# State term on 64x64 array tiles in a fused linear-attention and ELU feed-forward kernel

## The chip, the cores and the metric

The kernel runs on one core of a Trainium2 chip. The metric is device time in microseconds (us). Five engines matter. PE is TensorE, the matmul array; its weight loads are a lane of their own (PEld). DVE is VectorE, ACT is ScalarE, POOL is GpSimd and SP is SyncE. Each engine takes its own instructions in the order in which they were written, and semaphores tie the engines together. POOL and SP also issue DMA transfers: POOL all loads that cast from fp32 to fp16, SP the stores and the DMA transposes.

## The reference

There are two stages: a causal linear attention with a decay per head, and an ELU feed-forward layer on its output.

```
q, k, v: (4, 8, 768, 64)   lam: (8)   w_in: (512, 2048)   w_out: (2048, 512)
for each block of the sequence:
    intra = (q k^T * Dmask) v              Dmask[i,j] = lam^(i-j) for i >= j, else 0
    inter = (q * lam^(i+1)) state
    out   = intra + inter
    state = lam^block * state + (k * lam^(block-1-i))^T v
x = out as (3072 tokens, 512 = 8 heads x 64)
h = x w_in ;  g = ELU(h) ;  result = g w_out          (fp32)
```

## The kernel before, in words

The sequence is cut into 6 blocks of 128 tokens, times 4 batches: 24 groups. Group g has block g // 4 and batch g % 4. Eight heads are four pairs hp of two heads hh. For a group these steps exist, and a single letter names each in the written order of the program (`OPEN`, lines 53 to 62, and the loop at lines 613 to 634):

- T: q and k are transposed on PE (groups 0 to 7), or by DMA from SP (W, groups 8 on).
- S: the scores, 8 matmuls of 64 rows by 128 columns of the array (line 310). One bank of PSUM per hh. DVE multiplies them by the decay mask into `pp` (line 326).
- P: the attention output, transposed (x^T), into a PSUM bank `psO`. Per head pair there are two value matmuls (line 346; all 128 rows, 64 columns of the array each) and, from block 1 on, two state matmuls (line 352). The state of a batch is a 128x128 matrix per head pair with the two heads' 64x64 states on its diagonal and zeros beside them, so that a state matmul also takes all 128 rows and 64 columns. Then ACT (groups 0 to 7) or DVE (line 369, multiplying by `qs`) writes `psO` to `xt` in SBUF. A block of 128 rows of `xt` holds heads 2hp and 2hp+1.
- U: the state's new part, k^T v (line 405 for groups 0 to 3: four matmuls on the whole array; line 414 for the others: 16 matmuls of 128 rows by 64 columns for two groups), and two DVE instructions of 64 partitions that add it to the decayed old state (lines 424 and 426).
- M: the decayed old state, two POOL instructions of 64 partitions per group (line 386). kd (line 187) is POOL's decayed k.
- `1:g:j`: the first feed-forward matmul mm1 (line 493), ACT's exp and relu (499, 503), DVE's join into `g` (468). `2:g:j`: the second one, mm2 (line 517).
- z and Z: zeros written into the state matrices, four by DVE (line 210) and four by ACT (line 553), since the blocks beside the diagonal must be zero.

From group 4 on two groups make a burst: before, its order on PE is U, U, P, P in the loop and P, P, U, U in `OPEN`. The scores of the pair after are set ahead of the burst in the loop. The PSUM banks are given by tag; in the loop the two `psO` of a burst use the two banks "H" that mm1's results use in turn.

Loads: POOL's queue issues, in the order of `POOL_ORDER` (line 47), q, k and v of each group and the weights. `emit_wi` (line 166) loads a slice of w_in of 256 columns as one transfer over 128 partitions, with four row blocks of 128 of w_in. wi0 to wi7 are these slices, wo0 to wo7 those of w_out. The eight semaphores of POOL's transfers are used in turn, so that an issue also waits until the transfer issued eight before it has landed. Among the issues stand POOL's own kd and M.

Of the kernel before, what the change touches and what calls it, by code (L numbers as in the profile page):

```python
# [14 lines left out]
def kernel(  # L15
# [37 lines left out]
    OPEN = (  # L53
# [11 lines left out]
        "S0=M0,M1 S1=C,D S2=D,M1 S3=D,B P0=M1 P1=B P2=B P3=D U0=M0 U1=D U2=A U3=M1 T0=M1,C T1=D,A "  # L65
        "T2=A,D T3=D T4=M0 T5=A T6=M1 T7=D M2=C M3=M0"
    )
# [25 lines left out]
    for i in range(7):  # L93
# [22 lines left out]
    st = [  # L116
        [cpool.tile([128, NHP, 128], FP16, name=f"st{b}_{i}") for i in range(2)]
        for b in range(B)
# [47 lines left out]
    def emit_wi(i):  # L166
        f0 = sum(WI[:i]) * 128
        nc.gpsimd.dma_start(  # L168
            out=wi16[i][:],
            in_=moe_w_in[:, f0 : f0 + WI[i] * 128].rearrange("(k p) f -> p k f", p=128),  # L170
        )

# [35 lines left out]

    def zero_st1(b):
        nc.vector.memset(st[b][1][:], 0.0)  # L210


    loglam = cpool.tile([128, H], FP32, name="loglam")
# [7 lines left out]
    mask = cpool.tile([128, H, 128], FP32, name="mask")  # L221
    qs = cpool.tile([128, NHP, 128], FP32, name="qs")
    ks = cpool.tile([128, H], FP32, name="ks")
    upp = cpool.tile([128, NHP], FP32, name="upp")
# [10 lines left out]
    def emit_qs():  # L235
        for hh in range(2):
            r = slice(hh * 64, (hh + 1) * 64)
            nc.vector.tensor_copy(loglam_p[r, :], loglam[r, hh::2])
        for hp in range(NHP):
            nc.scalar.activation(  # L240
                qs[:, hp, :], row[:], AF.Exp, scale=loglam_p[:, hp : hp + 1]
            )

# [57 lines left out]

    def att_S(g):
        qt, kt = qkT[g]
        psS[g] = [
            bank(f"S{g}", hh, [128, NHP, 128], FP32, f"psS{g}_{hh}") for hh in range(2)
        ]
        for hp in range(NHP):
            for hh in range(2):
                r = slice(hh * 64, (hh + 1) * 64)
                nc.tensor.matmul(  # L310
                    psS[g][hh][:, hp, :], lhsT=kt[r, hp, :], rhs=qt[r, hp, :],
                    start=True, stop=True,
                )

    late, X_done, Y_done, E_done = [], set(), set(), set()

    def until(done, g):
        while g not in done:
            late.pop(0)()

    def att_E(g):
# [11 lines left out]
        return [lambda: half(0), lambda: half(1)]  # L333

    def att_P(g):
        cb, b = divmod(g, B)
        until(E_done, g)
        if cb > 0:
            until(Y_done, g - B)
        vt = of(vg, g)  # L340
        qt, _ = qkT[g]
        po = bank(f"P{g}", 0, [128, NHP, 128], FP32, f"psO{g}")
        R = [slice(0, 64), slice(64, 128)]
        for hp in range(NHP):
            for hh, r in enumerate(R):
                nc.tensor.matmul(  # L346
                    po[r, hp, :], lhsT=vt[:, 2 * hp + hh, :], rhs=Pt[(g, hh)][:, hp, :],
                    start=True, stop=(cb == 0), skip_group_check=True,
                )
            if cb > 0:  # L350
                for r in R:
                    nc.tensor.matmul(  # L352
                        po[r, hp, :], lhsT=st[b][cb % 2][:, hp, r], rhs=qt[:, hp, :],
                        start=False, stop=True, skip_group_check=True,
                    )

        def evacuate():
            g0 = GFIRST[g]
            n = GSIZE[g0]
            if g0 not in xg:  # L360
                xg[g0] = asb.tile(
                    [128, NHP, n * 128], FP16, tag=f"xt{n}", name=f"xt{g0}",
                    bufs=4 if n == 1 else 2,
                )
            dst = xg[g0][:, :, (g - g0) * 128 : (g - g0 + 1) * 128]
            if g < GPE:
                nc.scalar.copy(out=dst, in_=po[:])  # L367
            else:
                nc.vector.tensor_tensor(out=dst, in0=po[:], in1=qs[:], op=ALU.mult)  # L369
            X_done.add(g)  # L370

        return [evacuate]

    stt = {}

    def att_M(g):
        cb, b = divmod(g, B)
        if cb == NCB - 1:
            return
        assert f"U{g - B}" in seen  # L380
        until(Y_done, g - B)
        old = st[b][cb % 2]
        for hh in range(2):
            r = slice(hh * 64, (hh + 1) * 64)
            tmp = asb.tile([128, NHP, 64], FP32, tag="stt", name=f"stt{g}_{hh}", bufs=8)
            nc.gpsimd.tensor_tensor(  # L386
                out=tmp[r], in0=old[r, :, r],
                in1=upp[r].unsqueeze(2).broadcast_to([64, NHP, 64]), op=ALU.mult,
            )
            stt[(g, hh)] = tmp  # L390

# [4 lines left out]
    def att_U(g, pu=None):  # L396

        cb, b = divmod(g, B)
        if cb == NCB - 1:
            return []  # L400
        vt = of(vg, g)
        if pu is None:
            full = bank(f"U{g}", 0, [128, NHP, 128], FP32, f"psU{g}")
            for hp in range(NHP):
                nc.tensor.matmul(
                    full[:, hp, :].rearrange("p (h e) -> p h e", h=2),
                    lhsT=kds[g][:, 2 * hp : 2 * hp + 2, :],
                    rhs=vt[:, 2 * hp : 2 * hp + 2, :], start=True, stop=True,
                )
        else:  # L410
            for hp in range(NHP):
                for hh in range(2):
                    r = slice(hh * 64, (hh + 1) * 64)
                    nc.tensor.matmul(  # L414
                        pu[r, hp, :], lhsT=kds[g][:, 2 * hp + hh, :], rhs=vt[:, 2 * hp + hh, :],
                        start=True, stop=True, skip_group_check=True,
                    )
        new = st[b][(cb + 1) % 2]

        def update(hh):  # L420
            r = slice(hh * 64, (hh + 1) * 64)
            src = full[r, :, r] if pu is None else pu[r, :, :]
            if cb == 0:
                nc.vector.tensor_copy(new[r, :, r], src)
            else:
                nc.vector.tensor_tensor(  # L426
                    out=new[r, :, r], in0=stt.pop((g, hh))[r], in1=src, op=ALU.add
                )
            if hh == 1:
                Y_done.add(g)  # L430

        return [lambda: update(0), lambda: update(1)]

    def burst(*ops):

        us = [int(o[1:]) for o in ops if o[0] == "U" and int(o[1:]) // B < NCB - 1]
        evs, ups, i = [], [], 0
        for o in ops:
            if o[0] == "P":
                evs += att_P(int(o[1:]))  # L440
# [110 lines left out]

    def zero_st(b):
        nc.scalar.memzero(st[b][0][:])

    def load_pair(g):
# [11 lines left out]
    def ready(t):  # L567

        g = int(t[1:])
        if t[0] == "P":  # L570
            assert g < B or f"U{g - B}" in seen
        if t[0] == "U" and g < 2 * B:
            assert f"{'z' if g < B else 'Z'}{g % B}" in seen
# [4 lines left out]
    def run(t):  # L578
        w, *a = t[0], *t[1:].replace(":", " ").split()
# [5 lines left out]
        a = [int(x) for x in a]  # L585
        if w in "PUzZ":
            ready(t)
        if w == "S":
            for g in a:
                att_S(g)  # L590
            for g in a:
# [9 lines left out]
        else:  # L601
            {"T": att_T_pe, "1": mm1, "2": mm2, "Z": zero_st, "z": zero_st1,
             "q": lambda g, e: cast_raw(g, "q", e), "k": lambda g, e: cast_raw(g, "k", e),
             "c": lambda i: (emit_qs, emit_mask, emit_ks)[i](), "W": pool_work, "L": load_pair,
             "M": next_M, "w": zero_matmuls}[w](*a)

# [27 lines left out]
    prog += m2  # L634
    for t in prog:
        run(t)
    mm2_rest()
# [33 lines left out]
```

## Time and profile before

| | us |
|---|---|
| median of 3 runs (lowest to highest) | 213.92 (212.92 to 214.82) |
| the profiled execution | 213.1 |
| its span, first to last instruction | 211.3 |
| PE busy | 203.1 |
| DVE / ACT / POOL busy | 135.7 / 127.9 / 98.6 |
| mm1 on PE (line 493), mm2 (line 517) | 97.9, 95.3 |
| PE idle before 21.5 us, from there to 48.0, from there to 201.0 | 5.3, 0.1, 0.0 |

The profile's page gives busy time by engine, the span in 40 slices, the chain of work that ended last, and the costliest groups of instructions by line. Matmuls are pipelined, so that what one costs is read from the distance between starts, not from its duration. For a DMA, the issue on its queue and the landing are two different times.

### The profile page before, as it was taken

Reading aid. Unit: us, or ns where it says so; the run is one execution under the profiler, and the core shown is the slowest. Engines: PE = TensorE matmul, PEld = TensorE weight load, DVE = VectorE, ACT = ScalarE, POOL = GpSimd, SP = SyncE. Lnnn points to the kernel's source line nnn. Section 1 sums busy time; section 2 is a strip of 40 time slices with the busy share of each in tenths; the row PEclk is TensorE's granted clock in tenths of the full one; section 3 lists DMA queues with packets and bytes.
Section 4 is the critical chain, followed back from the end, with each engine's and each line's share of the span. In section 5 each row is a group of like instructions: output and inputs, shape, how many; then the busy total and the mean of one; then the engine's idle time right before and its main releaser. Section 6 shows DMA issues by size and latency. Waiting matters only on the chain.

```text
span 211.3 us, 5116 instructions
## 1 busy us (share of the span) xinstructions
PE 203.1 (96%) x2072; PEld 139.3 (66%) x2072; DVE 135.7 (64%) x233; ACT 127.9 (61%) x245; POOL 98.6 (47%) x113
## 2 busy tenths in 40 slices
PE   7597999999999999999999999999999999999994
PEld 2365677768686766776766766766766766666653
DVE  6966454687837888679677777676676764433320
ACT  2747555874867756676476476476476477577640
POOL 8998990999873969249195279200000000000000
DMA  8999999999997699993999939996620110110112
GB/s 106 160 183 192 190 167 186 124 161 150 153 161 126 100 220 153 187 141 27 164 114 137 164 99 87 181 150 86 126 76 0 53 50 0 54 50 8 44 50 99
DMA packets 103079, 24.71 MB, mean 117 GB/s; under 512 B 93200, under 2 KB 100624, under 8 KB 103056
## 3 DMA queue, kind: packets, MB, share of 16 engines
q0 software_dynamic: 79760, 13.50, 83.7%
q1 hardware_dynamic: 22768, 10.76, 27.1%
q8 instruction: 16, 0.26, 0.6%
q10 hardware_dynamic: 528, 0.13, 0.3%
q14 instruction: 7, 0.06, 0.1%
HBM read 27.40 MB, written 6.29 MB: 159 GB/s over the span
## 4 chain that ended last, share of the span: by engine, by line
PE 88%; POOL 6%; DMA 3%; issue 0%; DVE 0%; POOLq 0%
PE psM L517 39%; PE psH L493 39%; DMA wo<-in_moe_w_out_dram 3%; PE psS L310 3%; PE psO L346 3%; PE psO L352 2%; POOL wi L168 1%; POOL kn L129 1%; POOL qn L129 1%; POOL vn L129 1%; PE psU L414 1%; PE psT L291 1%; POOL kd L187 0%; PE psMrest L529 0%; POOL wo L175 0%
## 5 line engine op out<-in xcount | busy, mean ns | idle before, releaser
L493 PE MATMUL psH<-xt,wi 128*128 128x256 f16 (+1 forms) x896 | 97.9, 257 | 0.7 <-ACT xt L367 0.6
L517 PE MATMUL psM<-wo,g 128*128 128x512 f16 (+1 forms) x384 | 95.3, 377 | 0.9 <-DMA wo<-in_moe_w_out_dram 0.9
L499 ACT ACTIVATE e<-psH 128x512 f32<-128x512 f32 x96 | 57.4, 598 | 64.0 <-PE psH L493 63.9
L493 PEld LDWEIGHTS <-wi 128*128 128x128 f16 x896 | 77.2, 98 | 24.1 <-DVE g L468 0.9
L468 DVE SCALAR_TENSOR_TENSOR g<-e,r 128x512 f16<-128x512 f32 x64 | 47.2, 738 | 40.2 <-ACT r L503 39.7
L517 PEld LDWEIGHTS <-g 128*128 128x128 f16 x384 | 36.4, 98 | 29.2 <-issue 1.2
L503 ACT ACTIVATE r<-psH 128x512 f32<-128x512 f32 x64 | 38.1, 595 | 0.0
L326 DVE TENSOR_TENSOR pp<-psS,mask 128x512 f16<-128x512 f32 x48 | 30.8, 684 | 3.0 <-PE psS L310 2.7
L468 DVE SCALAR_TENSOR_TENSOR g<-e,psH 128x512 f16<-128x512 f32 x32 | 21.9, 685 | 14.4 <-ACT psH L503 14.1
L386 POOL TENSOR_TENSOR stt<-st,upp 64x256 f32<-64x256 f16 x32 | 21.6, 674 | 17.0 <-DVE st L426 10.8
L187 POOL TENSOR_TENSOR kd<-kn,ks 128x512 f16<-128x512 f16 x20 | 21.3, 1067 | 16.0 <-DMA kn<-in_k_dram 14.5
L503 ACT ACTIVATE psH<-psH 128x512 f32<-128x512 f32 x32 | 19.1, 596 | 0.0
L543 ACT COPY osb<-psM 128x512 f32<-128x512 f32 (+1 forms) x24 | 14.1, 589 | 5.2 <-PE psM L517 5.2
L129 POOL DMA_DIRECT2D kn<-in_k_dram x14 | 15.5, 1108 | 0.8 <-POOLq L655 0.8
L129 POOL DMA_DIRECT2D vn<-in_v_dram x14 | 15.5, 1105 | 0.6 <-DMA wi<-in_moe_w_in_dram 0.6
L129 POOL DMA_DIRECT2D qn<-in_q_dram x13 | 14.7, 1131 | 0.0
L426 DVE TENSOR_TENSOR st<-stt,psU 64x256 f16<-64x256 f32 x32 | 13.3, 417 | 1.2 <-PE psU L414 0.5
L346 PE MATMUL psO<-pp,vn 128*64 128x128 f16 x192 | 11.9, 221 | 0.2 <-DVE pp L326 0.2
L369 DVE TENSOR_TENSOR xt<-psO,qs 128x512 f16<-128x512 f32 x16 | 10.5, 685 | 2.4 <-PE psO L352 2.3
L346 PEld LDWEIGHTS <-vn 128*64 128x64 f16 x192 | 9.8, 110 | 2.8 <-issue 2.5
L352 PE MATMUL psO<-qT,st 128*64 128x128 f16 x160 | 10.1, 219 | 0.0
L310 PE MATMUL psS<-qT,kT 64*128 64x128 f16 x192 | 8.0, 218 | 1.1 <-ACT kT L299 1.0
(48 smaller groups left out, 89.6 us busy)
## 6 DMA issues: line engine op xcount, KB each, us to landing
out_dram<-osb SPq DMA_DIRECT2D x19, 256.0 KB, 3.5
kn<-in_k_dram POOLq DMA_DIRECT2D x10, 256.0 KB, 7.5
qn<-in_q_dram POOLq DMA_DIRECT2D x10, 256.0 KB, 7.9
vn<-in_v_dram POOLq DMA_DIRECT2D x10, 256.0 KB, 7.6
wi<-in_moe_w_in_dram POOLq DMA_DIRECT2D x8, 256.0 KB, 6.8
wo<-in_moe_w_out_dram POOLq DMA_DIRECT2D x8, 256.0 KB, 7.5
out_dram<-osb SPq DMA_DIRECT2D x8, 128.0 KB, 1.8
kn<-in_k_dram POOLq DMA_DIRECT2D x4, 128.0 KB, 5.1
```

Source lines behind the costliest of these rows:

```text
L129: nc.gpsimd.dma_start(out=t[:].rearrange("p b h d -> p (b h) d"), in_=src)
L187: nc.gpsimd.tensor_tensor(out=kd[:], in0=of(kg, g), in1=ks[:].unsqueeze(2).broadcast_to([128, H, 64]), op=ALU.mult,)
L310: nc.tensor.matmul(psS[g][hh][:, hp, :], lhsT=kt[r, hp, :], rhs=qt[r, hp, :], start=True, stop=True,)
L326: nc.vector.tensor_tensor(out=P[:], in0=pts[hh][:], in1=mask[:, hh::2, :], op=ALU.mult)
L346: nc.tensor.matmul(po[r, hp, :], lhsT=vt[:, 2 * hp + hh, :], rhs=Pt[(g, hh)][:, hp, :], start=True, stop=(cb == 0), skip_group_check=True,)
L352: nc.tensor.matmul(po[r, hp, :], lhsT=st[b][cb % 2][:, hp, r], rhs=qt[:, hp, :], start=False, stop=True, skip_group_check=True,)
L386: nc.gpsimd.tensor_tensor(out=tmp[r], in0=old[r, :, r], in1=upp[r].unsqueeze(2).broadcast_to([64, NHP, 64]), op=ALU.mult,)
L468: nc.vector.scalar_tensor_tensor(out=g[:].rearrange("p f c t -> p (f c t)"), in0=e[:], scalar=-1.0, in1=r[:], op0=ALU.add, op1=ALU.min,)
L493: nc.tensor.matmul(pH[:, f * n * 128 : (f + 1) * n * 128], lhsT=wi16[i][:, kk, w * 128 : (w + 1) * 128], rhs=xg[g0][:, kk, :], start=(kk = ...
L499: nc.scalar.activation(e[:], pH[:], AF.Exp)
L503: nc.scalar.activation(r[:], pH[:], AF.Relu)
L517: nc.tensor.matmul(psM[g][:, cols], lhsT=gts[(g, j * FB + f)], rhs=wo16[i][:, w, cols], start=first and f == 0, stop=end and f == FB - 1, ...
```

## The change

- The state of a head is a 64x64 block; a batch's state is 128 partitions by four head pairs by 64. There are no zeros to write, so z and Z go. M is one POOL instruction over 128 partitions, the state's update one DVE instruction.
- The state matmul takes 64 rows and 64 columns of the array. Four of them stand one after the other on the four quarters: rows by hh, columns by hp // 2. The two hh write two banks of PSUM, each of which now holds half of the heads of both groups of the burst.
- So a block of x^T holds heads k and 4+k. The rows of w_in must follow: each slice is loaded by two transfers of 64 partitions. The scaling at the evacuation uses a new table `qx` for the new order of heads (token x: two small DVE copies and four ACT exps).
- In a burst the state matmuls of both groups come first on PE, then the values (and U between them in the loop).
- U of groups 0 to 3 is eight matmuls of 128 rows by 64 columns in place of four on the whole array. Scores that stand right ahead of a burst (S14 to S23) are split into 64x64 tiles too: 16 matmuls per group in place of 8.
- The last burst's two `psO` use banks A and B in place of H.

```diff
-        nc.gpsimd.dma_start(
-            out=wi16[i][:],
-            in_=moe_w_in[:, f0 : f0 + WI[i] * 128].rearrange("(k p) f -> p k f", p=128),
-        )
+        for c in range(2):
+            nc.gpsimd.dma_start(
+                out=wi16[i][c * 64 : (c + 1) * 64],
+                in_=moe_w_in[c * 256 : (c + 1) * 256, f0 : f0 + WI[i] * 128].rearrange(
+                    "(k p) f -> p k f", p=64
+                ),
+            )
...
-    def att_S(g):
+    def att_S(g, split):
...
+        keys = [slice(0, 64), slice(64, 128)] if split else [slice(0, 128)]
         for hp in range(NHP):
             for hh in range(2):
                 r = slice(hh * 64, (hh + 1) * 64)
-                nc.tensor.matmul(
-                    psS[g][hh][:, hp, :], lhsT=kt[r, hp, :], rhs=qt[r, hp, :],
-                    start=True, stop=True,
-                )
+                for m in keys:
+                    nc.tensor.matmul(
+                        psS[g][hh][m, hp, :], lhsT=kt[r, hp, m], rhs=qt[r, hp, :],
+                        start=True, stop=True,
+                    )
...
+    def att_PP(g0):
+        pos2 = [
+            bank(f"P{g0 + hh}", 0, [128, 2, 2, 128], FP32, f"psO{g0}_{hh}") for hh in range(2)
+        ]
+        for c in range(2):
...
+            for s in range(2):
+                for hp in (s, s + 2):
+                    for hh in range(2):
+                        nc.tensor.matmul(
+                            pos2[hh][R[hp // 2], s, c, :], lhsT=st[b][cb % 2][R[hh], hp, :],
+                            rhs=qt[R[hh], hp, :], start=c == 0 and s == 0, stop=False,
+                            skip_group_check=True,
+                        )
+        def values():
+            for c in range(2):
...
+                for s in range(2):
+                    for hh in range(2):
+                        for hp in (s, s + 2):
+                            nc.tensor.matmul(
+                                pos2[hh][R[hp // 2], s, c, :], lhsT=vt[:, 2 * hp + hh, :],
+                                rhs=Pt[(g, hh)][:, hp, :], start=False, stop=True,
+                                skip_group_check=True,
+                            )
+        def evacuate(hh):
+            dst, src = x_of(g0)[:, hh::2, :], pos2[hh][:].rearrange("p s c t -> p s (c t)")
+            if g0 < GPE:
+                nc.scalar.copy(out=dst, in_=src)
+            else:
+                nc.vector.tensor_tensor(
...
-        for hh in range(2):
-            r = slice(hh * 64, (hh + 1) * 64)
-            tmp = asb.tile([128, NHP, 64], FP32, tag="stt", name=f"stt{g}_{hh}", bufs=8)
-            nc.gpsimd.tensor_tensor(
-                out=tmp[r], in0=old[r, :, r],
-                in1=upp[r].unsqueeze(2).broadcast_to([64, NHP, 64]), op=ALU.mult,
-            )
+        tmp = asb.tile([128, NHP, 64], FP32, tag="stt", name=f"stt{g}", bufs=4)
+        nc.gpsimd.tensor_tensor(
+            out=tmp[:], in0=st[b][cb % 2][:],
+            in1=upp[:].unsqueeze(2).broadcast_to([128, NHP, 64]), op=ALU.mult,
+        )
```

More of the change, by code (lines that the diff above doesn't have):

```diff
@@ L116 @@
     st = [
-        [cpool.tile([128, NHP, 128], FP16, name=f"st{b}_{i}") for i in range(2)]
+        [cpool.tile([128, NHP, 64], FP16, name=f"st{b}_{i}") for i in range(2)]
         for b in range(B)
@@ L241, in emit_qs, with emit_qx @@
                 qs[:, hp, :], row[:], AF.Exp, scale=loglam_p[:, hp : hp + 1]
+            )
+    def emit_qx():
+        for c in range(2):
+            r = slice(c * 64, (c + 1) * 64)
+            nc.vector.tensor_copy(loglam_x[r, :], loglam[r, c * NHP : (c + 1) * NHP])
+        for k in range(NHP):
+            nc.scalar.activation(
+                qx[:, k, :], row[:], AF.Exp, scale=loglam_x[:, k : k + 1]
             )
@@ L333, in att_E, with x_of @@
         return [lambda: half(0), lambda: half(1)]
+    R = [slice(0, 64), slice(64, 128)]
+    def x_of(g):
+        g0 = GFIRST[g]
+        n = GSIZE[g0]
+        if g0 not in xg:
+            xg[g0] = asb.tile(
+                [128, NHP, n * 128], FP16, tag=f"xt{n}", name=f"xt{g0}",
+                bufs=4 if n == 1 else 2,
+            )
+        return xg[g0]
     def att_P(g):
-        cb, b = divmod(g, B)
         until(E_done, g)
-        if cb > 0:
-            until(Y_done, g - B)
         vt = of(vg, g)
-        qt, _ = qkT[g]
@@ L402, in att_U, with update @@
         if pu is None:
-            full = bank(f"U{g}", 0, [128, NHP, 128], FP32, f"psU{g}")
-            for hp in range(NHP):
+            pu = bank(f"U{g}", 0, [128, NHP, 64], FP32, f"psU{g}")
+        for hp in range(NHP):
+            for hh in range(2):
                 nc.tensor.matmul(
-                    full[:, hp, :].rearrange("p (h e) -> p h e", h=2),
-                    lhsT=kds[g][:, 2 * hp : 2 * hp + 2, :],
-                    rhs=vt[:, 2 * hp : 2 * hp + 2, :], start=True, stop=True,
-                )
[L410 to L417, printed above, removed]
+                    pu[R[hh], hp, :], lhsT=kds[g][:, 2 * hp + hh, :], rhs=vt[:, 2 * hp + hh, :],
+                    start=True, stop=True, skip_group_check=True,
+                )
         new = st[b][(cb + 1) % 2]
-        def update(hh):
-            r = slice(hh * 64, (hh + 1) * 64)
-            src = full[r, :, r] if pu is None else pu[r, :, :]
+        def update():
             if cb == 0:
-                nc.vector.tensor_copy(new[r, :, r], src)
+                nc.vector.tensor_copy(new[:], pu[:])
             else:
[L426 to L432, printed above, removed]
+                nc.vector.tensor_tensor(out=new[:], in0=stt.pop(g)[:], in1=pu[:], op=ALU.add)
+            Y_done.add(g)
+        return [update]
     def burst(*ops):
@@ L438, in burst @@
         for o in ops:
+            if o[0] == "P" and int(o[1:]) >= B and int(o[1:]) % 2 == 0:
+                evs, values = att_PP(int(o[1:]))
+        for o in ops:
             if o[0] == "P":
-                evs += att_P(int(o[1:]))
+                g = int(o[1:])
+                if g < B:
+                    evs += att_P(g)
+                elif g % 2 == 0:
+                    values()
             elif int(o[1:]) in us:
@@ L576, in ready, with run @@
         seen.add(t)
-    def run(t):
+    def run(t, split=False):
         w, *a = t[0], *t[1:].replace(":", " ").split()
@@ L585, in run @@
         a = [int(x) for x in a]
-        if w in "PUzZ":
+        if w in "PU":
             ready(t)
@@ L589, in run @@
             for g in a:
-                att_S(g)
+                att_S(g, split)
             for g in a:
@@ L634 @@
     prog += m2
-    for t in prog:
-        run(t)
+    for t, following in zip(prog, prog[1:] + [""]):
+        run(t, split=following[:2] == "B:")
     mm2_rest()
```

63 lines of the change are left out of this document (29 added, 34 removed), and 6 rows, old and new, of the table OPEN.

## The prediction

> **What bounds the kernel now.** I read the page's busy times and 40 slices first, then busy time by stretch, then the chain that ended last in order of time.
>
> ```profile
> PE 203.1 (96%) x2072; PEld 139.3 (66%) x2072; DVE 135.7 (64%) x233; ACT 127.9 (61%) x245; POOL 98.6 (47%) x113
> PE   7597999999999999999999999999999999999994
> ...
> 21.50:48.00 26.50, 26.43 (x314) 18.73 (x313) 16.01 (x26) 17.10 (x32) 20.97 (x25) 1.00 1.64 165
> 48.00:95.00 47.00, 47.00 (x547) 33.97 (x547) 34.50 (x60) 31.33 (x60) 31.87 (x36) 1.00 1.63 154
> 95.00:201.00 106.00, 106.00 (x1003) 72.69 (x998) 68.02 (x108) 65.20 (x124) 26.09 (x27) 1.00 0.75 84
> ```
>
> The stretches' columns are length, then busy time of PE, weight loads, DVE, ACT and POOL, granted clock, DMA. From 21.5 us on PE has no idle time to speak of, at full clock. So there work taken from DVE, ACT or POOL buys nothing; only PE's own time and new PE waits count. Before that PE waits for loads, which the chain shows together with the list of POOL's instructions (start, length):
>
> ```profile
> 13.31 0.90 POOL qn L129
> 14.21 7.32 DMA wo<-in_moe_w_out_dram
> 21.57 0.59 PE psM L517 x2
> ...
> 17.29 1.46 POOL L175 DMA_DIRECT2D wo<-in_moe_w_out_dram x2
> 19.36 0.89 POOL L129 DMA_DIRECT2D vn<-in_v_dram  x1 [0.62 <-DMA wi<-in_moe_w_in_dram]
> 20.26 1.06 POOL L187 TENSOR_TENSOR kd<-kn,ks 128x512 f16<-128x512 f16 x1
> 21.27 1.30 POOL L386 TENSOR_TENSOR stt<-st,upp 64x256 f32<-64x256 f16 x2
> 22.65 2.21 POOL L187 TENSOR_TENSOR kd<-kn,ks 128x512 f16<-128x512 f16 x2
> 24.80 0.81 POOL L168 DMA_DIRECT2D wi<-in_moe_w_in_dram  x1
> 25.62 1.42 POOL L175 DMA_DIRECT2D wo<-in_moe_w_out_dram  x2
> 27.02 0.77 POOL L168 DMA_DIRECT2D wi<-in_moe_w_in_dram  x1
> ```
>
> POOL's queue runs without a pause from 1.25 to 31.5 us but for the 0.62 us shown. wo1, issued at 14.21, lands at 21.53, and PE waits for it. The last two w_in slices are wi7 (24.80, lands 29.91) and wi6 (27.02, lands 34.07). PE first uses both in the mm1 that starts at 34.73, only 0.66 us after wi6's landing. **The opening is a race between POOL's queue and PE that POOL barely wins.**
>
> **Part 1: eight more issues on POOL's queue.** Start to start an issue costs 0.75 us for wi (512 rows), 0.70 for wo (256 rows), 0.87 for k of one group (1024 rows), 1.15 for two groups (2048): mostly a fixed cost. Half a w_in slice has 256 rows, as wo has, so 0.70. A slice then costs 2 x 0.70 instead of 0.75: **+0.65**. Bounds: 0.375 per half (nothing added) to 0.75.
>
> wi7's first half is issued at 24.80 + 6 x 0.65 (wi0 to wi5) - 0.65 (line 386 once instead of twice) - 0.62 (v3's wait for a landing eight transfers back is over by then) = 27.4. The transfers issued before, the last of which landed at 28.51, will be nearly through, so the queue has to fill anew. wi7 took 5.1 us to land; with half the 1.3 us between landings of such slices, a half takes 4.45: halves at 31.9 and 32.55, against 29.91. wi6 landed 4.16 us behind wi7: 36.7. (Its second half is issued at 31.0, so the transfers, not the issue, set this.) PE reaches it at 34.73: **+2.0 us**. wo1 slips too (issue +2.6, landing some 0.5 later as its lead over the queue is used up), but that wait lies inside the 2.0: PE's delay is the largest of these, not their sum. Ends: 0 with nothing added per slice; with 0.75 per half and the full 5.1 us, wi7 ends at 33.8, wi6 at 37.95, +3.2. Later loads wait on POOL for PE's own U1 and move along.
>
> A rule of the Trainium skill speaks against this part: "DMA: Bandwidth & Descriptors", Rules for kernel authors, says of two transfers to disjoint partition halves "Don't bother — they serialize". By it two halves take as long on the DMA engines as one whole, which is what I assumed; no run here shows a half.
>
> **Part 2: PE's time per burst.** The order of PE around one burst of the loop:
>
> ```profile
> 102.27 0.62 PE L310 MATMUL psS<-qT,kT 64*128 64x128 f16 x16
> 102.82 0.44 PE L414 MATMUL psU<-vn,kd 128*64 128x64 f16 x16
> 103.09 0.23 PE L346 MATMUL psO<-pp,vn 128*64 128x128 f16 x2
> 103.15 0.22 PE L352 MATMUL psO<-qT,st 128*64 128x128 f16 x2
> 103.21 0.22 PE L346 MATMUL psO<-pp,vn 128*64 128x128 f16 x2
> ```
>
> Two value matmuls on the two column halves take 56 ns together (103.09 to 103.15 to 103.21), two state matmuls the same, and two score matmuls on the two row halves too: their starts lie 3 and 53 ns apart. No row shows four quarters at once. Lower bound: 56 ns, the pace of either pair. Next: U's pairs, with half the moving columns, still take 32 ns; were that the price of a load of 64 columns and row halves loaded one after the other, four would take 64. Upper: two pairs, 112. I take 56, since matmuls and loads of a pair start within 2 to 3 ns whichever way the array is cut.
>
> - State: 16 matmuls per burst, 8 pairs x 56 = 448 ns, become 4 x 56 = 224. Ten bursts: **-2.24** (64: -1.92; 112: 0).
> - Scores split, five pairs of groups: 8 pairs x 56 become 8 fours x 56: 0 (64: +0.32; 112: +2.24).
> - Changes of the array's cut: the last score matmul ahead of U has 146 to 148 ns where the others have 53, mm2 ahead of scores 959 where it has 864 elsewhere: 94 ns per change. In the order of instructions the changes of cut rise from 47 to 57 (one more in each burst without split scores, and around U1 to U3): **+0.94**.
> - U1 to U3: 223 ns for four whole matmuls become 8 at U's 17 ns: -0.09 each, **-0.26**.
>
> Sum: **-1.56** (64: -0.92; 112: +2.92).
>
> **Part 3: new waits, +0.3.** The state matmuls, now first in the burst, touch both H banks at once. ACT's relu of the mm1 before ends at 102.70; 60 ns after such an end PE starts, and the state matmuls would come at 102.72: 0.04 x 5 bursts = 0.2; behind them stand U, the values and mm2. The first P pair (48 us) fills both banks only at its end, so ACT's two copies end some 0.1 after PE reaches mm1 of group 4: 0.1. In the loop DVE's first evacuation is released 0.21 before mm2 starts, starts 0.24 later, takes 0.69 and is seen 0.06 later: 0.78 after mm2's start, against 0.87 when mm1 needs the bank. Free by 0.09; if DVE needs 0.1 more for the new pattern, each loop burst loses that.
>
> **Costed at nothing.** Zeros (DVE 1.1 us, ACT 1.4, at 8 to 9.8 us): PE's scores come some 0.9 us earlier, but then wo1 is late next. DVE's 20 updates less (0.42 each) and POOL's 16 (0.67, beyond the one above): behind a PE that is full. ACT's four exps (1.3 us, at 56 us) lie beside two mm2 of 0.86 each; without that cover the bank of the next mm1 would come up to 0.5 late. Evacuations keep count and size.
>
> **Sum**: +2.0 - 1.56 + 0.3 = **+0.7** on the profiled execution: 213.1 to 213.8. The median of the runs lies 0.8 above that execution, so 213.92 to **214.7**. A measurement of this kernel tells 1% (2.1 us) from no change.
>
> **Rivals.**
>
> 1. The extra issues are hidden or cheap. For: 0.66 of each issue is fixed only by a fit over whole transfers. Against: wo with as few rows still takes 0.70. Opening 0: -1.56 + 0.3, **212.7**.
> 2. The quarters don't run four at once, since the next four's weight loads wait for the row halves in use: 112 ns, so the change doesn't do what it says. For: no row shows four. Against: each kind of pair alone overlaps, and U's next load starts 26 ns after a matmul of 217 ns on the same rows. Part 2 turns into a loss at 75 ns per four (each ns costs 0.08 us over the 40 fours of state and 40 of scores); at 112: +2.0 + 2.92 + 0.3 = +5.2, **219.1**. The Trainium skill, "TensorE: Matmul & The Clock Gate", Part 3, The mechanism, says that weight loads overlap matmuls in flight only where the row group differs; by that rule this rival holds or worse, and the trace disagrees with it in U.
> 3. The opening slips by its upper end, and a four takes 64: +3.2 - 0.92 + 0.3 = +2.6, **216.5**. For: landing times grow to 9 us while the queue is full. Against: half as many bytes each.
>
> **How the numbers follow.** Forecast 0.55 (213.6 to 216.0), rival 1 0.15, rival 2 0.12, rival 3 0.15; 0.03 for what is not listed. The range 212.3 to 217.5 takes in all but rival 2 and the rest. Faster by over 1% would need -2.1, past the best sum of -1.3: 0.05. Slower by over 1%: rivals 2 and 3 and the upper edge of the forecast, 0.32. Within 1%: 0.63.
>
> **What would show it.** The list of POOL's instructions after: sixteen issues of w_in at 0.70 start to start, wi7's first at about 27.4. PE's waits: one for wi near 34.7 to 36.7, and one for wo near 21.5. In a burst the 16 state matmuls in 0.22 us; if they take 0.45, rival 2 holds. I am wrong if PE's wait before 37 us is under 1 or over 3 us, or if idle PE time shows after 50 us.

## The result, and the profile after

| | before | changed |
|---|---|---|
| median of 20 runs each, us | 213.44 | 214.36 |
| ratio, with its 95% interval | | 1.0046 (1.0027 to 1.0064) |
| span of the profiled execution, us | 211.3 | 212.6 |
| PE busy in it, us | 203.1 | 202.1 |
| end of PE's last multiplication, start of its span = 0 | 208.49 | 209.81 |

The changed kernel is slower by 0.5%, about 0.9 us; by the bound of 1% this is no change. The first profile of the changed kernel fell into a disturbed execution, so the lines here are of the same kernel profiled once more (run e1_after_again), and the ratios leave such executions out.

The page of the changed kernel, busy times and PE's row of the 40 slices, and busy time by stretch (columns: length, busy time of PE, weight loads, DVE, ACT and POOL, granted clock, DMA):

```profile
PE 202.1 (95%) x2168; PEld 137.0 (64%) x2168; DVE 124.9 (59%) x211; ACT 128.0 (60%) x245; POOL 91.6 (43%) x105
PE   7767897999999999999999999999999999999994
...
21.50:48.00 26.50, 24.66 (x311) 17.67 (x311) 13.57 (x22) 16.67 (x31) 22.26 (x26) 1.00 1.68 161
48.00:95.00 47.00, 46.48 (x533) 31.97 (x531) 31.53 (x55) 31.36 (x61) 25.66 (x27) 1.00 1.65 152
95.00:201.00 106.00, 106.00 (x1099) 72.75 (x1098) 64.26 (x101) 65.84 (x125) 23.80 (x23) 1.00 0.75 87
```

PE has 1.0 us less to do, DVE 10.8 and POOL 7.0 less. But PE now stands idle for 1.84 us between 21.5 and 48 us, where it stood 0.07 before, and for 0.52 us between 48 and 95, where it stood not at all. The two grew by 2.3 us together, which outweighs what PE saves. PE's waits over the whole span (time, times, longest):

```profile
PE psM L559 <- DMA wo<-in_moe_w_out_dram: 2.2, 2, 1.3
...
PE psH L535 <- DVE g L510: 0.4, 1, 0.4
PE psH L535 <- DMA wi<-in_moe_w_in_dram: 0.4, 1, 0.4
```

Before, PE waited once for wo, 0.9 us, and neither of the other two rows existed. The list of POOL's instructions around the first row's longer wait, and PE's own list there:

```profile
19.42 1.29 POOL L169 DMA_DIRECT2D wi<-in_moe_w_in_dram  x2
20.64 1.47 POOL L178 DMA_DIRECT2D wo<-in_moe_w_out_dram  x2
...
26.79 1.29 POOL L169 DMA_DIRECT2D wi<-in_moe_w_in_dram  x2
28.06 1.47 POOL L178 DMA_DIRECT2D wo<-in_moe_w_out_dram  x2
29.50 1.28 POOL L169 DMA_DIRECT2D wi<-in_moe_w_in_dram  x2
...
35.37 1.46 PE L559 MATMUL psM<-wo,g 128*128 128x512 f16 x6 [1.26 <-DMA wo<-in_moe_w_out_dram]
36.68 0.73 PE L535 MATMUL psH<-xt,wi 128*128 128x128 f16 x10
```

Two halves of a slice take 1.22 to 1.27 us of the queue where a whole one took 0.75. wo5, the second of the two issued from 28.06 on, lands at 35.33, and PE waits 1.26 us for it. wi6, at 29.50, lands at 36.63, just before PE needs it at 36.68.

I then followed single multiplications: the start of the same one in both kernels, and how far it has moved. Up to 36 us PE slips by 1.93 us. Behind that, each burst wins a little back, and two steps lose: +0.58 us at mm1 4:4 (59 us) and +0.26 us at mm1 6:6 (75 us). At the end 1.32 us are left. PE around one burst of the loop, changed kernel:

```profile
104.66 0.64 PE L322 MATMUL psS<-qT,kT 64*64 64x128 f16 x32
105.13 0.43 PE L391 MATMUL psO<-qT,st 64*64 64x128 f16 x16
105.49 0.44 PE L454 MATMUL psU<-vn,kd 128*64 128x64 f16 x16
105.77 0.62 PE L405 MATMUL psO<-pp,vn 128*64 128x128 f16 x16
106.32 0.39 PE L559 MATMUL psM<-wo,g 128*128 128x512 f16 x1
```

From the first score to mm2 this takes 1.66 us; before it took 1.82 (102.27 to 104.09).

### The profile page after: what moved, and what is told of

The parts are those of the page before. It is cut to its first block, busy times and chain, and to the rows that moved or that the text cites. A ratio compares the mean times of both kernels' runs of the same rounds, so it can differ in the third digit from the quotient of the medians.

```text
span 1161.3 us, 5250 instructions
## 1 busy us (share of the span) xinstructions
PE 1157.2 (100%) x2168; PEld 494.8 (43%) x2168; DVE 124.0 (11%) x211; ACT 132.0 (11%) x245; POOL 90.2 (8%) x105
## 4 chain that ended last, share of the span: by engine, by line
PE 100%; DVE 0%; issue 0%
PE psH L535 44%; PE psM L559 43%; PE psS L322 3%; PE psZ L84 3%; PE psO L405 2%; PE psT L301 2%; PE psU L454 1%; PE psO L391 1%; PE psO L368 0%; PE psMrest L571 0%; PE psCol L99 0%; DVE osb L583 0%; DVE zero L79 0%
## 5 line engine op out<-in xcount | busy, mean ns | idle before, releaser
L535 PE MATMUL psH<-xt,wi 128*128 128x256 f16 (+1 forms) x896 | 535.8, 946 | 0.0
L559 PE MATMUL psM<-wo,g 128*128 128x512 f16 (+1 forms) x384 | 530.4, 1684 | 0.0
L535 PEld LDWEIGHTS <-wi 128*128 128x128 f16 x896 | 276.3, 317 | 322.4 <-issue 313.8
L559 PEld LDWEIGHTS <-g 128*128 128x128 f16 x384 | 118.8, 313 | 263.1 <-issue 260.8
L322 PEld LDWEIGHTS <-kT 64*64 64x64 f16 (+1 forms) x272 | 22.6, 271 | 23.5 <-issue 22.7
L322 PE MATMUL psS<-qT,kT 64*64 64x128 f16 (+1 forms) x272 | 32.4, 654 | 0.0
L84 PE MATMUL psZ<-zero 128*128 128x512 f16 x23 | 30.9, 1666 | 1.2 <-DVE zero L79 1.2
L405 PE MATMUL psO<-pp,vn 128*64 128x128 f16 x160 | 27.9, 671 | 0.0
L454 PE MATMUL psU<-vn,kd 128*64 128x64 f16 x160 | 16.5, 427 | 0.0
L391 PE MATMUL psO<-qT,st 64*64 64x128 f16 x160 | 15.6, 666 | 0.0
```

The costliest lines, as they stand in the source:

```text
L84: nc.tensor.matmul(z[:], lhsT=zero16[:, 0:128], rhs=zero16[:], start=True, stop=True)
L322: nc.tensor.matmul(psS[g][hh][m, hp, :], lhsT=kt[r, hp, m], rhs=qt[r, hp, :], start=True, stop=True,)
L391: nc.tensor.matmul(pos2[hh][R[hp // 2], s, c, :], lhsT=st[b][cb % 2][R[hh], hp, :], rhs=qt[R[hh], hp, :], start=c == 0 and s == 0, stop=False,
L405: nc.tensor.matmul(pos2[hh][R[hp // 2], s, c, :], lhsT=vt[:, 2 * hp + hh, :], rhs=Pt[(g, hh)][:, hp, :], start=False, stop=True, skip_grou ...
L454: nc.tensor.matmul(pu[R[hh], hp, :], lhsT=kds[g][:, 2 * hp + hh, :], rhs=vt[:, 2 * hp + hh, :], start=True, stop=True, skip_group_check=True,)
L535: nc.tensor.matmul(pH[:, f * n * 128 : (f + 1) * n * 128], lhsT=wi16[i][:, kk, w * 128 : (w + 1) * 128], rhs=xg[g0][:, kk, :], start=(kk = ...
```

## The experiments

Times are medians, each with runs of the kernel before on the same chip beside it, whose medians lay at 213.05 to 213.16 us. Ratios are to those, with 95% intervals. "PE's shift" is the movement of the same multiplication against the kernel before.

### The opening: is it the issues?

**e1_after_again** is the changed kernel.

> The changed kernel as it is, for a profile of it at full clock and its time in these rounds. Theory A (the forecast): the opening costs about 2.0 us, PE's bursts give back about 1.6, new waits take 0.3; 0.7 to 1.0 us above the kernel before. In its profile PE waits about 2 us in all for wi or wo between 21 and 37 us, and 16 state matmuls take 0.22 us. Theory B: the opening costs little, and the extra time comes from waits or changes of cut in the bursts; then PE's waits before 37 us are as before, and idle or lengthened PE time shows behind 48 us.

Measured: 214.33 us, 1.0047 (1.0029 to 1.0065); its lines are above.

**e2_halves_only**: the kernel before, with nothing changed but w_in's transfers.

```diff
-        nc.gpsimd.dma_start(
-            out=wi16[i][:],
-            in_=moe_w_in[:, f0 : f0 + WI[i] * 128].rearrange("(k p) f -> p k f", p=128),
-        )
+        src = moe_w_in[:, f0 : f0 + WI[i] * 128].rearrange("(k p) f -> p k f", p=128)
+        for c in range(2):
+            r = slice(c * 64, (c + 1) * 64)
+            nc.gpsimd.dma_start(out=wi16[i][r], in_=src[r])
```

> The kernel before with one part of the change alone: each w_in slice in two transfers of 64 partitions, with the rows where they were. Theory A: PE waits for wi6 or wo5, 2.0 us above the kernel before (0.9 to 3.2), with M still two POOL instructions, so 0.6 more than in the changed kernel: 2.0 to 2.6. Theory B: under 0.7 us above it.

Measured: 215.38 us, 1.0109 (1.0088 to 1.0130), so +2.3 us. In its profile, of an execution of 214.84 us, PE slips by 1.45 us at the mm2 that waits for wo4 and wo5 and by 1.74 in all, and the bursts are as before. The split of the loads alone costs what the whole opening was forecast to cost.

**e3_one_transfer**: the changed kernel with one transfer per slice. The rows of w_in keep their old order, so that mm1 multiplies some heads with other heads' rows; the work is the same in kind and amount.

```diff
-        for c in range(2):
-            nc.gpsimd.dma_start(
-                out=wi16[i][c * 64 : (c + 1) * 64],
...
+        nc.gpsimd.dma_start(
+            out=wi16[i][:],
+            in_=moe_w_in[:, f0 : f0 + WI[i] * 128].rearrange("(k p) f -> p k f", p=128),
+        )
```

> The changed kernel with each w_in slice in one transfer of 128 partitions. The rows of w_in then stand in the old order, so that the feed-forward layer multiplies the heads of x^T with rows of other heads; everything else is kept. Theory A: without the opening's delay the bursts' gain is left, 1.3 us under the kernel before (0.6 to 1.6). Theory B: 0.3 to 1 us above it, as the changed kernel.

Measured: 212.34 us, 0.9965 (0.9952 to 0.9979): 0.77 us faster than before, 2.0 faster than the changed kernel. The stretch from 21.5 to 48 us is full again:

```profile
21.50:48.00 26.50, 26.50 (x334) 18.62 (x337) 14.93 (x24) 16.78 (x31) 20.63 (x23) 1.00 1.77 174
48.00:95.00 47.00, 46.62 (x540) 32.80 (x542) 31.31 (x52) 32.37 (x63) 25.43 (x28) 1.00 1.64 150
```

So the opening's loss belongs to the second issues, shown from both sides. PE's first mm1 starts 0.42 us earlier here, where no zeros are written, and of that 0.03 to 0.15 is left from 35 to 40 us: the early start is given back to the loads, as costed. But 0.38 us of idle time stay between 48 and 95 us, and the steps at 59 and 75 us (+0.45 and +0.26) with them. They have nothing to do with loads.

**e4_wide_halves**: four w_in slices of 512 columns, two halves each, so eight issues again.

```diff
-    WI = [2] * 8
+    WI = [4] * 4
...
+        s, c = divmod(i, 2)
...
```

> The changed kernel with w_in in four slices of 512 columns in place of eight of 256, each in two transfers of 64 partitions: eight issues on POOL's queue as before, each of the same bytes, in the same places. All of the computation is kept. Theory A (it is the number of issues that delays the opening): 1.3 us under the kernel before (0.4 to 1.6). Rival: transfers of 64 partitions are slow in themselves; then it stays above the kernel before by 0.5 us or more, and wi6 lands later than 34.1 us although its issue is not late.

Measured: 213.51 us, 1.0015 (0.9988 to 1.0042), its runs spread from 212.4 to 216.5: 0.4 above the kernel before and not 1.3 under it. The profiled execution was the longest of the twelve, and shows a cost of another kind. The page's row of the granted clock, busy time by stretch, and PE's list:

```profile
PEclk9985699999999999999999999999999999999999
...
10.00:14.00 4.00, 2.37 (x25) 1.06 (x22) 1.77 (x3) 0.12 (x1) 3.95 (x6) 1.00 1.89 174
14.00:26.00 12.00, 10.35 (x108) 8.92 (x106) 4.28 (x7) 6.19 (x12) 9.33 (x13) 0.57 1.46 195
...
13.42 0.64 PE L367 MATMUL psO<-pp,vn 128*64 128x128 f16 x16 [1.64 <-DMA vn<-in_v_dram]
15.42 0.82 PE L534 MATMUL psH<-xt,wi 128*128 128x128 f16 x6 [0.70 <-DMA wi<-in_moe_w_in_dram]
```

The first mm1 has to wait for twice the data (the second half lands at 15.38), and v0, queued behind the first half, lands at 13.38 instead of the 12.11 of the kernel before. PE is idle for 1.64 and 0.70 us, and the clock granted from 14 to 26 us is 0.57: multiplications run every 113 ns instead of 56. In that execution fewer issues of larger pieces trade one loss for another. The clock does not explain the other runs: nine of the twelve had a mean of 0.999 or more and still took 212.4 to 215.2 us, and what spread them is not shown. Nor is the rival settled: the last half of w_in, issued at 27.17, landed at 34.75, where the whole slice of the kernel before, with the same bytes and issued at 27.02, landed at 34.07.

### The bursts: what does the split of the scores bring?

**e6_scores_whole**: the changed kernel with whole scores ahead of the bursts.

```diff
-        run(t, split=following[:2] == "B:")
+        run(t)
```

> The changed kernel with the scores ahead of a burst left on 64x128 tiles, 8 matmuls per group. Theory A (a four of 64x64 tiles costs the same 56 ns as a pair, and each change of the array's cut 94 ns): five changes more, 0.35 to 0.47 us above the changed kernel's 214.33. Rival (four tiles cost 64 ns or more): the split scores cost 0.3 us or more, which this run gives back, so that it stays within 0.15 us of the changed kernel.

Measured: 214.51 us, 1.0066 (1.0054 to 1.0078), 0.18 us above the changed kernel, which is between the two theories, and its interval overlaps that of the changed kernel. The starts on PE tell more:

```profile
104.32 0.62 PE L322 MATMUL psS<-qT,kT 64*128 64x128 f16 x16
104.87 0.42 PE L391 MATMUL psO<-qT,st 64*64 64x128 f16 x16
105.22 0.44 PE L454 MATMUL psU<-vn,kd 128*64 128x64 f16 x16
```

Sixteen whole scores take 0.55 us up to the state's first start, thirty-two split ones 0.47 (above): with the split the change of cut between scores and state is gone. Each loop burst wins 0.100 us against before, where the split one wins 0.168: 0.34 over five, just under the forecast for it.

### The two new waits

At 59 us PE waits for DVE's join of mm1 4:2, which frees a bank. DVE, POOL and PE of the changed kernel:

```profile
58.75 0.68 DVE L338 TENSOR_TENSOR pp<-psS,mask 128x512 f16<-128x512 f32 x1
59.35 1.01 DVE L248 COPY loglam_x<-loglam 64x4 f32<-64x4 f32 x2
60.40 0.69 DVE L510 SCALAR_TENSOR_TENSOR g<-e,psH 128x512 f16<-128x512 f32 x1
...
59.13 1.03 POOL L190 TENSOR_TENSOR kd<-kn,ks 128x512 f16<-128x512 f16 x1
...
61.14 1.03 PE L535 MATMUL psH<-xt,wi 128*128 128x256 f16 x8 [0.42 <-DVE g L510]
```

Token x puts two copies of four numbers per partition ahead of the join. The first takes 0.83 us, the second 0.17. My first theory was that x merely stands at a bad place.

**e5_x_early**: token x behind `2:0:0`, in the opening.

```diff
-        ... 1:0:1 2:0:0 "
+        ... 1:0:1 2:0:0 x "
...
-        ... S6:7 1:4:2 x 2:4:0 ...
+        ... S6:7 1:4:2 2:4:0 ...
```

> The changed kernel with the table qx made 36 us earlier (token x behind the first mm2 of group 0, where PE waits for wo1, in place of behind the mm1 4:2). Theory A, from the changed kernel's trace: the two DVE copies for qx stand ahead of DVE's join of mm1 4:2 and hold up the bank that mm1 4:4 writes, 0.58 us; without them there the time falls by 0.5 to 0.6 us against the changed kernel's 214.33 and PE has no idle time there. Rival: the banks are short there in any case, since both banks of x^T are now held to the end of the burst; then PE still waits at 59 to 61 us and the time stays.

Measured: 217.56 us, 1.0208 (1.0195 to 1.0222). The step at 59 us is gone, and one of 3.6 us stands at 26. Behind it the granted clock is half for 3.4 us, in which PE's shift grows by another 1.5 us; the mean clock was 0.992 in all five runs. PE's wait, the stretch behind it, and DVE and POOL:

```profile
29.69 1.64 PE L535 MATMUL psH<-xt,wi 128*128 128x128 f16 x16 [3.46 <-DVE g L510]
...
29.97:33.37 3.40, 3.40 (x37) 3.01 (x35) 2.32 (x5) 1.67 (x3) 3.40 (x5) 0.50 1.13 155
...
22.05 4.59 DVE L248 COPY loglam_x<-loglam 64x4 f32<-64x4 f32 x2
...
21.92 0.89 POOL L129 DMA_DIRECT2D vn<-in_v_dram  x1 [0.30 <-DMA wo<-in_moe_w_out_dram]
22.82 1.06 POOL L190 TENSOR_TENSOR kd<-kn,ks 128x512 f16<-128x512 f16 x1
23.82 0.62 POOL L435 TENSOR_TENSOR stt<-st,upp 128x256 f32<-128x256 f16 x1
24.39 2.03 POOL L190 TENSOR_TENSOR kd<-kn,ks 128x512 f16<-128x512 f16 x2
```

The first copy runs for 4.41 us and ends at 26.46, when POOL's four tensor instructions have run out (24.39 + 2.03 = 26.42); the second takes 0.17. The 3.6 us are not the copy's alone: behind the copies ACT's four exps of x (from 26.68, 1.28 us) stand ahead of ACT's part of mm1, so that DVE's join starts only at 28.94. When the first copy starts, POOL is still issuing the load of v. The first of the two copies of `loglam_p` at 6.14 us, of the same form, seems to wait for an issue too: it takes 0.38 us in the kernel before and 0.26 in the changed one, and ends within 0.01 us of the issue that POOL has under way (6.53 and 6.40). So the new theory: a copy from SBUF to SBUF on DVE waits while POOL works, on tensors above all. The Trainium skill, "SBUF — State Buffer", Who interferes with whom, says that DVE and GpSimd share one pair of ports as an exclusive lock, that a DVE copy can take it, and that `tensor_reduce` on this chip never does. That gives a test in which nothing moves.

**e9_copy_as_reduce**: the changed kernel; x stays where it was.

```diff
-            nc.vector.tensor_copy(loglam_x[r, :], loglam[r, c * NHP : (c + 1) * NHP])
+            nc.vector.tensor_reduce(
+                out=loglam_x[r, :],
+                in_=loglam[r, c * NHP : (c + 1) * NHP].unsqueeze(2),
+                op=ALU.add, axis=mybir.AxisListType.X,
+            )
```

> The changed kernel, with the two DVE copies of loglam_x written as tensor_reduce over an axis of length one; they stand at the same place in DVE's order and give the same values. In the changed kernel these copies took 0.168 and 0.833 us, and the second one ended 0.2 us after a kd product on POOL (59.13 to 60.16); the join behind them came 0.58 us late to PE. Theory A (a shared port: a float32 SBUF-to-SBUF copy on DVE waits until POOL's instruction is over, an operation of another kind does not): both take 0.1 to 0.25 us, the step of +0.58 us at the first multiplication 4:4 falls to at most 0.25, the time falls by 0.3 to 0.6 us to 213.7 to 214.0, with the step of +0.26 us at the sixth feed-forward bank still there. Rival B (it is the place in the queue, or DVE is slower whenever POOL works): the two take about 1.0 us as before, the step stays, the time is 214.3.

Measured: 213.73 us, 1.0014 (0.9986 to 1.0041), 0.6 us under the changed kernel. DVE and POOL:

```profile
58.42 0.68 DVE L343 TENSOR_TENSOR pp<-psS,mask 128x512 f16<-128x512 f32 x1
59.02 0.30 DVE L248 TENSOR_REDUCE loglam_x<-loglam 64x4 f32<-64x4 f32 x2
59.36 0.69 DVE L515 SCALAR_TENSOR_TENSOR g<-e,psH 128x512 f16<-128x512 f32 x1
...
58.85 1.03 POOL L190 TENSOR_TENSOR kd<-kn,ks 128x512 f16<-128x512 f16 x1
```

Beside the same kd on POOL the two reduces take 0.30 us instead of 1.01, and the step at 59 us is gone from PE's shift altogether. Theory A holds, the rule of the Trainium skill with it; place in the queue does not explain it.

The second step, at 75 us: DVE's first evacuation of burst P8 stands ahead of the join that frees the next bank of mm1. DVE in the kernel before, then in the changed one:

```profile
73.65 0.69 DVE L369 TENSOR_TENSOR xt<-psO,qs 128x512 f16<-128x512 f32 x1 [0.86 <-PE psO L352]
74.26 0.69 DVE L468 SCALAR_TENSOR_TENSOR g<-e,psH 128x512 f16<-128x512 f32 x1
```

```profile
76.30 0.69 DVE L416 TENSOR_TENSOR xt<-psO,qx 128x512 f16<-128x512 f32 x1 [1.16 <-PE psO L405]
76.91 0.68 DVE L510 SCALAR_TENSOR_TENSOR g<-e,psH 128x512 f16<-128x512 f32 x1
```

Before, the first group's bank was full after that group's own attention, and its evacuation ran beside the second group's. Now each bank takes half the heads of both groups and is full only at the end of all values. The evacuation starts at 76.30, behind all values; the join could start when ACT's relu ends, at 76.58, and goes behind it at 76.91.

**e7_join_first**: e5 plus the join ahead of the evacuation in two bursts.

```diff
+        if ops[0] in ("P8", "P10"):
+            flush()
         for e in evs:
             e()
```

> The kernel of e5 with DVE's waiting join put ahead of the first evacuation in the bursts of groups 8 and 10. Theory A: in the changed kernel the evacuation waits for both groups' values, the join stands behind it on DVE and frees the bank of mm1 6:6 0.26 us late; with the join first that is gone, another 0.2 to 0.3 us under e5. Rival: the evacuation then comes later and mm1 of group 8 waits for it instead, the same time as e5.

Measured: 217.22 us, 1.0130 (1.0084 to 1.0176), still under x's 3.6 us in the opening. Its six runs spread from 214.1 to 218.3 us, so the time says nothing on 0.26 us. In the profile the step at 75 us is gone.

**e8_fewer_issues**: e7 with w_in slices of 2, 2, 4, 4 and 4 blocks, ten issues, the first two slices small so that mm1 can start.

```diff
-    WI = [2] * 8
+    WI = [2, 2, 4, 4, 4]
...
-        for c in range(2):
+        s, halves = (i, (0, 1)) if i < 2 else (2 + (i - 2) // 2, (i % 2,))
+        for c in halves:
```

> The kernel of e7 with w_in in two slices of 256 columns and three of 512, each in two transfers of 64 partitions: ten issues on POOL's queue where the changed kernel has sixteen and the one before has eight. Theory A: two issues more move wo1 and the last slices by less than their lead, so the opening's 1.9 us go as well: 1.2 to 1.7 us under the kernel before (about 211.6). Rival, from e4: transfers of 64 partitions land later in themselves or the first matmuls come late and the clock falls; then it is less than 0.8 us under the kernel before.

Measured: 212.87 us, 0.9994 (0.9976 to 1.0012), 0.18 us under the kernel before and not 1.2 to 1.7. PE's shift behind the opening is +1.0 us, of which +0.58 is x again; its two copies took only 1.05 us together in this order of POOL's, and ACT's four exps follow them.

**e10_both_waits_out**: e9 and the join first; x at its place.

> The run above, and in bursts P8 and P10 the pending feed-forward join goes ahead of the first evacuation. Theory A (the two new waits, 0.58 and 0.26 us, are what ate the gain, and nothing else lies behind them): about 0.7 to 0.85 us under the changed kernel, 213.5, and PE's shift against the kernel before is about +1.9 us after the opening and falls to about +0.5 at the end. Rival B (another wait comes up in their place): under 0.4 us gained, 213.9 or more, with a new step in PE's shift elsewhere.

Measured: 213.36 us, 1.0000 (0.9977 to 1.0023), 0.97 us under the changed kernel. The stretch from 48 to 95 us:

```profile
48.00:95.00 47.00, 47.00 (x540) 32.85 (x539) 31.79 (x55) 31.85 (x62) 26.99 (x29) 1.00 1.63 158
```

No idle time is left there, and no new step appears. PE's shift is +1.75 us behind the opening and +0.26 at the end: the loss that remains is the loads.

**e11_best** and **e12_best_twelve**: e10 with slices of 2, 2, 4, 4, 4 blocks (ten issues), and of 2, 2, 2, 2, 4, 4 (twelve).

> The run above with w_in slices of 2, 2, 4, 4 and 4 blocks, so 10 issues in place of 16. Theory A (the opening costs by the number of issues on POOL's queue before w_out slice 5: about +0.45 us left of +1.9, the bursts give -1.35, the two waits are gone): 0.7 to 1.0 us under the kernel before, 212.1 to 212.4, ratio 0.995 to 0.997. Rival B (the larger slices make PE idle in the opening so that the granted clock falls, as with slices of four from the start): clock under 0.99 and over 213.

> The run before, with w_in slices of 2, 2, 2, 2, 4 and 4 blocks: 12 issues in place of 10, and the halves of the third slice again issued one behind the other. In the run before, PE's first multiplication of the third slice stood until its second half had landed at 19.95 us, PE's shift there was +0.96 us, and the granted clock fell for one slice of the span behind it. Theory A (that wait made the loss of +1.46 us in the opening, and four issues more than in the kernel before cost at most 1.0 us): shift at most +1.0 us behind the opening, clock 1.0, the end 0.4 to 0.9 us before the kernel before, 212.1 to 212.7, ratio 0.994 to 0.998. Rival B (every issue more costs in full until w_out's slice 5, and the two issues more take what the earlier half brings): shift +1.5 us or more, ratio 0.998 or more.

Measured: 212.74 us, 0.9964 (0.9934 to 0.9994), and 212.46 us, 0.9977 (0.9958 to 0.9995). Both are faster than either kernel by a little, and their PE ends 0.04 and 0.05 us before the kernel before. In the profiled executions neither opening came out as meant: the shift behind it is +1.46 and +1.44 us. In e11, PE waits until 19.95 us for the second half of the third slice, which is now issued behind other loads, and the clock of the first 21.5 us is 0.98, of the next stretch 0.96. In e12 the clock is 1.00 and the shift at 34 us only +0.39, but then PE waits for the last half of w_in, issued at 27.25 and landed at 36.05; PE goes on at 36.18. PE's shift in e12 comes near rival B, though by another mechanism than it names; the time and its ratio lie where A had them. Why that half took 8.8 us where wi6, issued at 27.02 in the kernel before, took 7.05 was not settled. Openings of single executions differ, too: e9 and e10, with the same loads as the changed kernel, have slipped by 1.62 and 1.75 us at 40 us, where it has by 1.95, so differences of 0.3 us there carry no weight.

Both profiles are of executions longer than the median (213.08 and 213.09 us). Of e11's ten runs, the six with a mean clock of 0.991 or 0.992 took 212.7 to 213.8 us, and the four with 0.999 or more 211.6 to 211.9. These four are 1.3 to 1.6 us under the kernel before, about what PE's own time gives, although their loads come in halves too. So ten issues can leave the opening nearly without a loss; what is lost in the other six goes with the clock.

## Why the prediction was right, point by point

The forecast was +0.7 us, and the runs gave +0.9. The sum was made for the profiled execution, though, whose span grew by 1.3 us: the opening and the bursts came out nearly as forecast, and the new waits cost 0.84 us in place of 0.3, at other places than those named.

1. **What bounds the kernel: right.** All that was won or lost is PE's own time and PE's waits; DVE's 10.8 and POOL's 7.0 us less of work show in the time at one place, with 0.10 us (point 4).
2. **Opening, +2.0: right (1.93), with its parts off.** An issue of a half takes 0.60 to 0.67 us, not 0.70. wi7's halves land 3.25 and 3.44 us after their issue, not 4.45, so at 30.0 and 30.9. But wi6 lands at 36.63, against 36.7 forecast, since it stands behind two wo transfers, of which the second landed 2.2 us after the first. That wi7 came 1.66 us earlier than forecast and wi6 1.58 us further behind it, so that the two errors cancel, is luck. The profile shows the wait at wo5, six multiplications earlier; wi6 would have set the same time. What carried the forecast was to follow the queue to the last landing.
3. **The rule on two partition halves** (the Trainium skill, "DMA: Bandwidth & Descriptors", Rules for kernel authors: they serialize) agrees with the trace: wi6's halves land 0.62 and 0.68 us behind the transfer ahead of each, 1.30 in all, as a whole slice took. What hurt is the queue: e2 costs 2.3 us for the second issues alone.
4. **PE's bursts, -1.56: too large, -1.38.** Fours of 64x64 tiles start every 55 to 56 ns, so rival 2 is out, and with it the rule of the Trainium skill in "TensorE: Matmul & The Clock Gate", Part 3, The mechanism, as I read it: by that rule a four would take 112 ns here. A loop burst wins 0.17 us where 224 ns less for the state alone was forecast; about 0.04 of the difference is that the starts within a four of the state are staggered, over 25 ns in the first and 48 in the last, where those of the scores lie within 10. Bursts with a change of cut more win 0.10, where 0.224 - 0.094 = 0.13 was forecast. U1 to U3, -0.26 in the forecast, give nothing: +0.12 is taken back by -0.13 a little later. A further 0.10 us, at the first mm2 of group 12, is a small delay of the kernel before that is gone. That mm2 writes the bank in which U of groups 14 and 15 stood, and DVE's updates of the state free it. In the kernel before, DVE's two updates (L426) run from 124.31 to 125.17, and PE's mm2 starts at 125.23, 0.21 us behind the multiplication ahead of it instead of 0.11. In the changed kernel the updates (L464) start at 123.23 and are over 3 us before that mm2.
5. **New waits, +0.3: the wrong ones.** None of those named (H banks 0.2, the first P pair 0.1) shows. Two others do, with 0.58 + 0.26 = 0.84 us. The step that failed is "Costed at nothing". It priced token x by ACT's four exps, and named "up to 0.5 late" for the bank of the next mm1, but let the two DVE copies go by as small; the profile had only two of that form, of 0.38 and 0.17 us, made while POOL had no tensor work. And "Evacuations keep count and size" missed that they change their time: I looked at the loop, where the join is not behind them, and not at P8's kind of burst in `OPEN`. e9 and e10 show that both waits can be had out, with nothing behind them.
6. **What would make it wrong**: PE's wait before 37 us stayed between 1 and 3 us, but idle time does show after 50 us, 0.52 us of it. By its own test the forecast was wrong there, and right in its sum.

The sum as measured, with the shift of 1.95 us that is left behind the opening: +1.95 - 1.38 - 0.10 + 0.84 = +1.31, against +1.32 at PE's last multiplication. Rival 1 (cheap issues) fell with e2, rival 2 with the list of PE's starts, and rival 3 with both.

## What to carry to other kernels

When an edit splits a load, count its issues on the queue and follow them to the landing of the last transfer that the busy engine waits for; here eight issues more, of 0.60 to 0.67 us each, ate all that faster multiplications gave. When it changes which results share a bank, ask when each bank is full, and what stands behind its evacuation on that engine. And price a small instruction by what its neighbours do at that moment: four numbers per partition cost 0.17 us or 4.4.

## What the runs showed of the hardware

- A DVE copy of 64x4 fp32 from SBUF to SBUF took 0.17, 0.83 and 4.41 us, by how long POOL went on; as a reduce it took 0.14 and 0.15. In e5 it did not come in between POOL's instructions but waited for four of them, back to back. In e4 one did come in: it ended at 61.38, 0.03 us behind one POOL instruction, though the next had started, and the copy behind it then took 0.99 us. The Trainium skill ("SBUF — State Buffer", SBUF: two separate sides) tells of a lock held for a whole instruction; that a waiting copy can be passed over several times is this trace's addition.
- In e5 the granted clock was 0.50 for 3.4 us behind an idle stretch of PE of 3.46 us. The longest execution of e4 had 0.50 from 14.8 to 25.0 us behind idle stretches of 1.64 and 0.70 us, and e11's profiled one 0.50 for 3.4 us from 20.45 on, when PE had been busy for 1.50 of the 3.41 us before, with no gap over 1.1. The Trainium skill ("TensorE: Matmul & The Clock Gate", Why this matters for your kernels) asks for no idle gaps over about 3 us; e5 agrees, and in e4 and e11 the clock fell without one as long.
- In the changed kernel a half slice landed 3.25 us after its issue at 26.79, with three transfers ahead of it that were all down by 29.07, and another 6.45 us after its issue at 29.50, with four ahead, the last down at 35.33.
